# Three stages on one core: v read in 512-byte runs with a swap of key halves, and expert matrices loaded in halves during attention

## The chip, the cores and the metric

The kernel runs on 1 core of a Trainium2 chip. The metric is the device time in microseconds of one execution on that core. All loads and stores are issued by SyncE (SP), in program order, on one DMA queue that 16 DMA engines serve.

## What is computed

Chunked attention over 8 batches, 8 heads, 576 positions and a head size of 64 (chunks of 64 positions attend to themselves alone), then a soft mixture of 8 experts with 4 slots each over all 4608 tokens, then a block of two matrices with softplus between them.

```python
scores = scale * q_c @ k_c^T                      # per chunk of 64
attn = exp(scores - max); attn /= sum + 1e-09
x = attn @ v_c                                    # -> (4608, 512) tokens
logits = x @ phi                                  # 32 slots
d = softmax of logits over the tokens             # dispatch
slot_out[e] = relu((d.T @ x)[e] @ w1[e]) @ w2[e]  # 8 experts, w1: 512x1024, w2: 1024x512
x = softmax of logits over the slots @ slot_out   # combine
out = softplus(x @ w_in) @ w_out                  # 512x2048 and 2048x512
```

## The kernel before

**Attention** runs in 36 units of two heads and 512 positions: 9 groups `G` of four units. Group 0 (`MIXED`) collects the last 64 positions of all batches, group G the first 512 of batch G-1. For a unit, PE transposes q and k (`A0`, `A1`; line 404), ScalarE copies them to the tile `T` (`B`, line 413), GpSimd copies each half of `T` to the other 64 partitions (`M`, line 421), PE makes the scores (`S`, line 435), VectorE takes maximum and difference (`m0`, `m1`; lines 446 and 452), ScalarE the exponential (`x`, line 460), PE transposes the probabilities (`C`, line 468), ScalarE or VectorE copies them back (`Ce`, line 473), PE multiplies them with v (`D`, line 487, into `X`), VectorE normalizes (`n0`, `n1`; lines 501 to 510), PE transposes the result (`E`, line 522) and an engine copies it (`Ee`, line 529). Once a group, `F` (line 540) makes logits and `Fy` (line 598) sums tokens into the slots.

v is loaded for two units at once (`lv`, a pair of units, 512 KB; line 270): four DMAs, one for each block of 128 positions, whose runs in DRAM are one row of 64 floats, that is 256 bytes. Partition p of block m holds position 128m + p. There are three buffers for v; a column of ones behind each head's 64 makes the sum of the probabilities come out of `D`.

**Experts.** `w1` and `w2` have 16 pieces of 1 MB each. `H` n (line 926) multiplies the slots with piece n of w1, `SO` n (line 967) the hidden values with piece n of w2. The pieces lie in slots of SBUF: `w0` to `w7` (each two tiles of 512 KB, loaded by two DMAs), `g0` to `g3` and `i0` to `i3` (one DMA of 1 MB), and `d0` to `d4`, which exist only when the pools of attention are closed, so they wait for the last `A1`, `S` and `D`. Slots are used again: `H` 0 frees `w0` for piece 5 of w2, and so on; `w_in` and `w_out` follow in the slots that come free (`AFTER`).

**What sets the order.** The order on each engine is fixed when the program is built. `issue` keeps a clock for each engine, adds for each step the cost that `COST` lists and a latency, and takes the step that can begin first (at the same time, by rank). Loads of expert pieces (`lw`) have a high rank, so they fill SP's clock where no load of attention can begin. On the chip every engine then works through its list in order, and a step that waits holds up all that stand behind it on its engine.

**After the experts** come `soT`, `Td` (lines 986, 1007) and then 72 blocks of `h` (line 1078), softplus (lines 1097 to 1117) and `o` (lines 1134 to 1138). Beside the experts, three batches of combine weights are made (`c1` to `c6` on VectorE, ScalarE and GpSimd, then `d`, transposes of line 850, and `dc`, copies of line 856), and w_in and w_out are split into two parts each (lines 333 to 350, 872 to 883).

Of the kernel before, what the change touches and what calls it, by code (L numbers as in the profile page):

```python
# [64 lines left out]
class Step:  # L65
    def __init__(self, nm, key, fn, deps, take, give, rank, cost=None, after=()):
# [4 lines left out]
        self.urgent = False  # L71


def issue(steps, buffers, clock=None, held=None):
# [26 lines left out]
    while n:  # L101
# [30 lines left out]
        s.end = clock[e] + LATENCY[e]  # L132
# [10 lines left out]
def kernel(  # L143
# [98 lines left out]
    vb = [vb2[:, i].rearrange("p (m h e) -> p m h e", m=4, e=VW) for i in range(2)]  # L242
    vb += [ap.tile([128, 4, 4, VW], F32, name=f"vb{i}") for i in range(2, NV)]
# [40 lines left out]
    def load(nm, n, sl):  # L284
# [9 lines left out]
        parts = halves(sl)  # L294
        if sl[0] == "w":
            for t, x in zip(parts, (src[:, 0], src[:, 1])):
                nc.sync.dma_start(out=t.bitcast(U32) if nm == "wo" else t, in_=x)
# [83 lines left out]
    def st_lv(pr):  # L381
        def f(e, held):
            if pr // 2 == MIXED:
                assert held["v", pr] == pr
                V["v", pr] = vm[:, :, 4 * pr:4 * pr + 4]
                if pr == 0:
                    load_vm()
                return
            V["v", pr] = vb[held["v", pr]]
            load_v(V["v", pr], pr)  # L390
# [33 lines left out]
    def st_S(u):  # L424
        def f(e, held):
# [4 lines left out]
            for i in range(4):  # L430
                for b in range(2):
                    for h in range(2):
# [3 lines left out]
                            out=sp[64 * o:64 * o + 64, b, 64 * i:64 * i + 64],  # L436
# [12 lines left out]
    def st_m1(u):  # L449
        def f(e, held):  # L450
            t = V["P", u] = ap.tile([128, 4, 128], F32, tag=f"P{held['P', u]}", name="P")
            nc.vector.tensor_tensor(  # L452
# [23 lines left out]
    def st_D(u):  # L476
        def f(e, held):
            xp = V["X", u] = psa.tile([128, 2, 512], F32, tag="X", name="X")
            pt, vt = V.pop(("P", u)), V["v", u // 2]
            for i in range(2):  # L480
                for h in range(2):
                    for b in range(2):
                        m = 2 * b + i
                        for c in range(2):
                            o = c ^ b
                            a = 64 * (h ^ b)
                            nc.tensor.matmul(  # L487
# [916 lines left out]
```

## Time and profile before

| what | us |
|---|---|
| three runs | 680.23, 681.58 (median), 685.54 |
| the profiled execution | 681.11 |
| its span, first to last instruction | 679.3 |
| PE busy over the span | 635.1 |
| VectorE, ScalarE, GpSimd busy | 428.7, 335.6, 237.5 |
| DMA: bytes moved | 107.93 MB, 159 GB/s mean |

Shares of busy time are means over stages that differ: the span has an attention stage (to about 160 us), an expert stage (to about 225 us), a start of the last stage (to about 290 us) and the rest of it. What ends last is read in each stage apart.

### The profile page before, as it was taken

What the parts mean: (1) busy time and instruction counts of PE and PEld (TensorE: products, weight loads), DVE (VectorE), ACT (ScalarE), POOL (GpSimd) and SP (SyncE); (2) the same over time, 40 slices, a digit from 0 to 9 for tenths busy, and PEclk for the clock granted to TensorE, in tenths of its full rate; (3) what the DMA queues carried; (4) which work ended last, traced back from release to release, by engine and by line L of the source; (5) the groups of instructions that cost most, each with busy time, mean ns of one, the idle gap of its engine ahead of it and who ended that gap; (6) DMA issues with size and microseconds to landing.
All of it is one profiled execution on the core that took longest, in us unless ns stands there. A gap on an engine that the chain in (4) does not pass through costs nothing.

```text
span 679.3 us, 14080 instructions
## 1 busy us (share of the span) xinstructions
PE 635.1 (93%) x5831; PEld 510.1 (75%) x5831; DVE 428.7 (63%) x630; ACT 335.6 (49%) x511; POOL 237.5 (35%) x205
## 2 busy tenths in 40 slices
PE   6899889978984899999999999999999999999997
PEld 5787777865352577878788788888888888888885
DVE  1778778774247589878887777754455554545551
ACT  2565656642046589645555865553333333333330
POOL 4233223220214536612222234444333444433341
PEclk7999999998898789999999999999999999999999
DMA  9799989899999802102412510122414223231312
GB/s 176 195 259 257 262 241 271 219 315 418 415 409 415 323 31 95 61 31 99 150 62 90 221 62 32 59 97 73 113 63 123 64 81 106 78 110 63 119 36 62
DMA packets 80255, 107.93 MB, mean 159 GB/s; under 512 B 42432, under 2 KB 60864, under 8 KB 78016
## 3 DMA queue, kind: packets, MB, share of 16 engines
q1 hardware_dynamic: 80192, 107.04, 48.5%
q8 instruction: 46, 0.75, 0.5%
q14 instruction: 17, 0.14, 0.1%
HBM read 88.15 MB, written 18.87 MB: 158 GB/s over the span
## 4 chain that ended last, share of the span: by engine, by line
PE 72%; DMA 13%; DVE 8%; issue 2%; ACT 2%; POOL 2%; SPq 1%; POOLq 0%; DVEq 0%; ACTq 0%
PE trm L1134 17%; PE trm L1136 17%; PE trm L1138 17%; DMA i<-in_moe_w_dram 5%; PE ph L1078 4%; PE tr L404 3%; PE X L487 2%; PE S L435 2%; DMA d<-in_moe_w_dram 2%; PE tr L468 2%; DMA g<-in_moe_w_in_dram 2%; PE tr L522 2%; DMA w5b<-in_moe_w_dram 1%; DMA w3b<-in_moe_w_dram 1%; PE tr L540 1%
## 5 line engine op out<-in xcount | busy, mean ns | idle before, releaser
L1117 POOL TENSOR_TENSOR g<-hTm,g 128x1024 fp32r<-128x1024 f32 (+1 forms) x37 | 87.4, 2363 | 111.7 <-ACT g L1113 107.9
L1103 ACT ACTIVATE hTm<-hTm 128x1024 f32<-128x1024 f32 (+2 forms) x51 | 51.4, 1010 | 78.4 <-DVE hTm L1097 78.1
L1097 DVE TENSOR_SCALAR hTm<-ph 128x1024 uint32<-128x1024 uint32 (+2 forms) x51 | 59.0, 1158 | 35.0 <-PE ph L1078 34.9
L421 POOL COPY T<-T 64x512 f32<-64x512 f32 x72 | 43.9, 610 | 99.7 <-ACT T L413 98.9
L1107 DVE SCALAR_TENSOR_TENSOR hTm<-ph,hTm 128x1024 f32<-128x1024 f32 (+1 forms) x37 | 44.2, 1195 | 25.6 <-ACT hTm L1103 25.5
L1113 ACT CAST g<-hTm 128x1024 fp32r<-128x1024 f32 (+1 forms) x37 | 38.0, 1027 | 40.0 <-DVE hTm L1107 40.0
L1150 DVE TENSOR_TENSOR i<-trm,i 128x512 f32<-128x512 f32 x52 | 35.7, 687 | 31.9 <-PE trm L1138 31.8
L413 ACT COPY T<-tr 128x512 f32<-128x512 f32 x72 | 40.9, 588 | 23.3 <-PE tr L404 23.2
L1078 PEld LDWEIGHTS ph<-cT,Tc 128*128 128x128 f32 x288 | 43.7, 190 | 11.4 <-issue 4.4
L1078 PE MATMUL ph<-cT,Tc 128*128 128x256 f32 x288 | 47.0, 286 | 2.4 <-DVE g L1117 1.2
L1097 DVE TENSOR_SCALAR siT<-ph 128x1024 uint32<-128x1024 uint32 (+1 forms) x25 | 29.5, 1181 | 25.6 <-PE ph L1078 25.5
L1103 ACT ACTIVATE siT<-siT 128x1024 f32<-128x1024 f32 (+1 forms) x25 | 25.7, 1027 | 38.5 <-DVE siT L1097 38.5
L1117 POOL TENSOR_TENSOR g<-siT,g 128x1024 fp32r<-128x1024 f32 x12 | 28.9, 2408 | 42.5 <-ACT g L1113 42.5
L1117 DVE TENSOR_TENSOR g<-ph,g 128x1024 fp32r<-128x1024 f32 (+2 forms) x27 | 29.6, 1102 | 10.0 <-ACT g L1113 10.0
L404 PE MATMUL tr<-ident,q 128*128 128x128 f32 x144 | 29.1, 284 | 5.7 <-DMA q<-in_q_dram 4.3
L446 DVE TENSOR_REDUCE nm<-S 128x8 f32<-128x512 f32 x36 | 24.7, 686 | 14.7 <-PE S L435 14.6
L1113 ACT CAST g<-ph 128x1024 fp32r<-128x1024 f32 (+2 forms) x27 | 24.7, 919 | 18.2 <-DVE ph L1107 16.8
L435 PE MATMUL S<-T 64*64 64x64 f32 x1152 | 25.2, 225 | 6.0 <-DVE P L452 2.8
L435 PEld LDWEIGHTS S<-T 64*64 64x64 f32 x1152 | 21.1, 137 | 12.0 <-issue 7.2
L460 ACT ACTIVATE P<-P 128x512 f32<-128x512 f32 x36 | 23.0, 638 | 11.5 <-DVE P L452 11.4
L404 PE MATMUL tr<-ident,k 128*128 128x128 f32 x144 | 28.3, 279 | 0.3 <-DMA k<-in_k_dram 0.3
L452 DVE TENSOR_TENSOR P<-S,nm 128x512 f32<-128x512 f32 x36 | 24.5, 681 | 2.1 <-PE S L435 1.3
(453 smaller groups left out, 1766.7 us busy)
## 6 DMA issues: line engine op xcount, KB each, us to landing
part<-i SPq DMA_DIRECT2D x18, 512.0 KB, 2.6
i<-part SPq DMA_DIRECT2D x18, 512.0 KB, 3.6
q<-in_q_dram SPq DMA_DIRECT2D x32, 256.0 KB, 4.7
k<-in_k_dram SPq DMA_DIRECT2D x32, 256.0 KB, 4.6
i<-in_moe_w_dram SPq DMA_DIRECT2D x7, 1024.0 KB, 15.5
vbm<-in_v_dram SPq DMA_DIRECT2D x40, 128.0 KB, 4.7
g<-in_moe_w_dram SPq DMA_DIRECT2D x5, 1024.0 KB, 7.9
d<-in_moe_w_dram SPq DMA_DIRECT2D x5, 1024.0 KB, 13.4
```

The source lines that it names most:

```text
L404: nc.tensor.transpose(c, t[:, h, 2 * rr:2 * rr + 2, :].rearrange("p r d -> p (r d)"), ident)
L421: nc.gpsimd.tensor_copy(out=t[a:a + 64, :, 1], in_=t[b:b + 64, :, 2 * h])
L435: nc.tensor.matmul(out=sp[64 * o:64 * o + 64, b, 64 * i:64 * i + 64], lhsT=cs[:, 0], rhs=cs[:, 1], start=True, stop=True)
L1078: nc.tensor.matmul(out=ph(n, a, b)[:, j - a, :], lhsT=K["Tc"][:, f * 128:(f + 1) * 128], rhs=K["cT"][:, t * TT:(t + 1) * TT], start=True, ...
L1097: nc.vector.tensor_scalar(out=scratch(n, a, b).bitcast(U32), in0=ph(n, a, b).bitcast(U32), scalar1=0x80000000, scalar2=None, op0=ALU.bitwi ...
L1103: nc.scalar.activation(out=y, in_=y, func=AF.Softplus)
L1107: nc.vector.scalar_tensor_tensor(out=soft(n, a, b), in0=ph(n, a, b), scalar=0.0, in1=y, op0=ALU.max, op1=ALU.add)
L1113: nc.scalar.copy(out=V["gs", n][:, 0, a:b], in_=soft(n, a, b))
L1117: tt(e)(out=s[:, 1, a:b], in0=soft(n, a, b), in1=s[:, 0, a:b].bitcast(F32), op=ALU.subtract)
L1134: nc.tensor.matmul(out=po, lhsT=s[:, 0, j, ts_], rhs=wr[:, hs], start=(n in begin and j == 0), stop=False)
L1136: nc.tensor.matmul(out=po, lhsT=s[:, 0, j, ts_], rhs=wr[:, ls], start=False, stop=False)
L1138: nc.tensor.matmul(out=po, lhsT=s[:, 1, j, ts_], rhs=wr[:, hs], start=False, stop=(j == 3 and n in finish))
```

## The change

For all groups but `MIXED`, v is read in runs of two rows (512 bytes): two DMAs for a pair of units in place of four, each over 256 positions, with positions 256b + 2p and 256b + 2p + 1 on partition p. A chunk's keys then don't lie where the scores of that chunk have them, so new steps `N` exchange 32 partitions of one of the two rows with 32 of the other, through a buffer of the `xT` tiles: six copies for a pair of units, four on GpSimd and two on ScalarE, one after the other, and `D` waits for them. The order of chunks in `S`, `m1`, `D` and in the stores follows from the new layout; the permuting write in `m1` goes away. The planner's cost of `lv` falls from 2.7 to 2.1, and 2.5 us are added to the time at which it takes v to be there. Each expert piece of the first 11 of w1 that don't wait for attention's pools, and the first five of w2, is loaded as two steps of 512 KB with a cost of 1.35 each (before: one step of 2.6); g and i slots, too, are now filled by two DMAs.

```diff
-    "lq": {"SP": 1.7}, "lv": {"SP": 2.7}, "lwi": {"SP": 1.35},
+    "lq": {"SP": 1.7}, "lv": {"SP": 2.1}, "lwi": {"SP": 1.35},
...
+"N": {"POOL": 0.65},
...
-        s.end = clock[e] + LATENCY[e]
+        s.end = clock[e] + LATENCY[e] + s.lag
...
-        for m in range(4):
+        for b in range(2):
             nc.sync.dma_start(
-                out=t[:, m, :, 0:D],
-                in_=v[batch_of(G), h0:h0 + 4, 128 * m:128 * m + 128, :].rearrange(
-                    "h p d -> p h d"))
+                out=t[:, b, :, 1:2 * D + 1],
+                in_=v[batch_of(G), h0:h0 + 4, 256 * b:256 * b + 256, :].rearrange(
+                    "h (p r) d -> p h (r d)", r=2))
...
+    def st_N(pr, n):
+        def f(e, held):
+            t = V["vt", pr]
+            if n == 0:
+                V["vs", pr] = xp_.tile([128, 512], F32, tag=f"xT{held['xT', ('N', pr)]}", name="xT")
+            vtmp = V["vs", pr].rearrange("p (b h d) -> p b h d", b=2, h=4)
+            i, n_ = divmod(n, 3)
+            lo, up = slice(64 * i, 64 * i + 32), slice(64 * i + 32, 64 * i + 64)
+            dst, src = ((vtmp[lo], t[up, :, :, 1:1 + D]),
+                        (t[up, :, :, 1:1 + D], t[lo, :, :, 1 + D:VW + D]),
+                        (t[lo, :, :, 1 + D:VW + D], vtmp[lo]))[n_]
+            if e == "ACT":
+                nc.scalar.copy(out=dst, in_=src)
+            else:
+                nc.gpsimd.tensor_copy(out=dst, in_=src)
...
+            by["lv", pr].lag = 2.5
+            for n in range(6):
+                add("N", (pr, n), st_N(pr, n), [("lv", pr)] + [("N", (pr, n - 1))] * (n > 0),
...
+                    {"ACT": 0.6} if n % 3 == 2 else {"POOL": 0.67})
...
-        add("D", u, st_D(u), [("Ce", u), ("lv", pr)],
+        add("D", u, st_D(u), [("Ce", u), ("lv", pr), ("N", (pr, 2)), ("N", (pr, 5))],
...
+    def halved(nm, n, sl, r):
+        add("lw", (nm, n, 0), at(load, nm, n, sl, 0), rank=r, cost={"SP": 1.35})
+        add("lw", (nm, n), at(load, nm, n, sl, 1), [("lw", (nm, n, 0))], rank=r, cost={"SP": 1.35})
...
-            add("lw", ("w1", n), at(load, "w1", n, sl), rank=100 + n)
+            halved("w1", n, sl, 100 + n)
     for n in range(5):
-        add("lw", ("w2", n), at(load, "w2", n, W2[n]), rank=130 + n)
+        halved("w2", n, W2[n], 130 + n)
...
-        if t % 2 == 0 and G != MIXED:
-            nc.sync.dma_start(out=out[rows[0]:rows[0] + 128, :], in_=o)
-            return
```

SP, the last loads of attention, before. `w0`, `w1`, `g0`, `g1` and `g2` (5 MB of expert pieces, the last of them in the first row) stand ahead of the last v (vb and vbm are the buffers of v), and `w2a` follows on it:

```order
L300 DMA g2_2789<-in_moe_w1_dram 128x2048
L263 DMA q_2834<-in_q_dram 128x2x256
L263 DMA k_2835<-in_k_dram 128x2x256
L270 DMA vb2_116<-in_v_dram 128x4x64 x4
L297 DMA w2a_2930<-in_moe_w1_dram 128x1024
L297 DMA w2b_2931<-in_moe_w1_dram 128x1024
L297 DMA w3a_3007<-in_moe_w1_dram 128x1024
L297 DMA w3b_3008<-in_moe_w1_dram 128x1024
```

SP, the same place now (line 300 is an expert piece, 264 q and k, 271 v):

```order
L300 DMA w5a_2703<-in_moe_w1_dram 128x1024
L271 DMA vbm_115<-in_v_dram 128x4x128 x2
L264 DMA q_2778<-in_q_dram 128x2x256
L264 DMA k_2779<-in_k_dram 128x2x256
L300 DMA w5b_2704<-in_moe_w1_dram 128x1024
L300 DMA w6a_2860<-in_moe_w1_dram 128x1024
L264 DMA q_2906<-in_q_dram 128x2x256
L264 DMA k_2907<-in_k_dram 128x2x256
L271 DMA vb2_116<-in_v_dram 128x4x128 x2
L300 DMA w6b_2861<-in_moe_w1_dram 128x1024
L302 DMA g3_3024<-in_moe_w1_dram 128x1024
```

Nine more DMAs of 512 KB (`w2a` to `w6a`) stand ahead of the last load of v than before.

GpSimd in the middle of attention, before (line 421 is `M`, two for a unit):

```order
L421 COPY T_798<-T_798 64x16x32 x2
L421 COPY T_855<-T_855 64x16x32 x2
L421 COPY T_943<-T_943 64x16x32 x2
L421 COPY T_1015<-T_1015 64x16x32 x2
L421 COPY T_1113<-T_1113 64x16x32 x2
```

GpSimd in the middle of attention, now (line 447 is `M`, line 414 is `N`, which reads or writes a buffer of v):

```order
L414 COPY xT_1567<-vb2_116 32x512
L447 COPY T_1558<-T_1558 64x16x32
L414 COPY vb2_116<-vb2_116 32x8x64
L447 COPY T_1558<-T_1558 64x16x32
L447 COPY T_1585<-T_1585 64x16x32
L414 COPY xT_1567<-vb2_116 32x512
L447 COPY T_1585<-T_1585 64x16x32
L414 COPY vb2_116<-vb2_116 32x8x64
L447 COPY T_1675<-T_1675 64x16x32 x2
L414 COPY xT_1743<-vbm_115 32x512
```

The copies that the scores wait for now stand in one list with the copies that wait for v.

PE at the start of the last stage, before (line 986 is `soT`, 1007 `Td`, 1078 `h`, 1134 to 1138 `o`; the three groups of the last batch of combine weights, line 850, stand further ahead, among the `SO`):

```order
L986 MATMUL trm_3827<-rep_60,ts 128x128 x2
L1007 MATMUL trm_3846<-g_3639,soT 128x128 x4
L1007 MATMUL trm_3855<-g_3639,soT 128x256 x4
L1078 MATMUL ph<-cT,Tc 128x256
L1007 MATMUL trm_3875<-g_3639,soT 128x128 x4
L1078 MATMUL ph<-cT,Tc 128x256 x7
L1134 MATMUL trm_3915<-w0a,g_3908 128x512
L1136 MATMUL trm_3915<-w0a,g_3908 128x512
```

PE at the same place now (line 1029 is `soT`, 1050 `Td`, 1121 `h`, 893 the transposes of combine weights, 1177 `o`):

```order
L1029 MATMUL trm_3897<-rep_60,ts 128x128 x2
L1050 MATMUL trm_3915<-g_3614,soT 128x128 x4
L1050 MATMUL trm_3921<-g_3614,soT 128x256 x4
L1121 MATMUL ph<-cT,Tc 128x256
L1050 MATMUL trm_3941<-g_3614,soT 128x128 x4
L893 MATMUL trm_3949<-ident,cr 128x128 x4
L1121 MATMUL ph<-cT,Tc 128x256 x2
L893 MATMUL trm_3963<-ident,cr 128x128 x4
L1121 MATMUL ph<-cT,Tc 128x256 x3
L893 MATMUL trm_3980<-ident,cr 128x128 x4
L1121 MATMUL ph<-cT,Tc 128x256 x2
L1177 MATMUL trm_4003<-w0a,g_3997 128x512
```

The three groups of the last batch have moved from among the `SO` to among the first `h`.

## Rows read from the trace of the kernel before

**Rows 1.** Windows of five stages; first row: what the columns are

```profile
core 0: us, PE busy (x) PEld busy (x) DVE busy (x) ACT busy (x) POOL busy (x), PEclk, DMA share, GB/s
14.00:158.00 144.00, 129.47 (x3093) 106.99 (x3095) 108.57 (x243) 83.85 (x179) 42.72 (x70) 0.98 0.90 257
144.00:174.00 30.00, 24.98 (x408) 17.97 (x402) 14.87 (x40) 9.11 (x23) 4.53 (x5) 0.90 1.02 402
174.00:223.00 49.00, 37.37 (x418) 18.63 (x410) 22.96 (x39) 22.39 (x36) 13.18 (x9) 0.92 1.02 412
223.00:235.00 12.00, 9.77 (x56) 7.69 (x56) 5.96 (x14) 6.49 (x15) 4.73 (x4) 0.74 0.96 380
235.00:290.00 55.00, 52.83 (x234) 41.45 (x234) 48.85 (x65) 45.73 (x74) 28.69 (x19) 0.94 0.17 58
```

**Rows 2.** Chain of waits in order of time (start us, us, what)

```profile
143.90 8.01 DMA w3b<-in_moe_w_dram
...
208.05 15.07 DMA i<-in_moe_w_dram
223.17 1.98 PE sops L967 x16
```

**Rows 3.** Timeline of SP's queue (start us, us)

```profile
58.76 0.46 SPq L297 DMA_DIRECT2D w0a<-in_moe_w_dram  x1
...
133.67 0.46 SPq L300 DMA_DIRECT2D g<-in_moe_w_dram  x1
...
135.72 6.22 SPq L270 DMA_DIRECT2D vb<-in_v_dram  x4
142.00 0.91 SPq L297 DMA_DIRECT2D w2a<-in_moe_w_dram  x1
...
174.21 0.33 SPq L297 DMA_DIRECT2D w0a<-in_moe_w_dram  x1
```

**Rows 4.** Timeline of PE (start us, us): four places

```profile
160.41 0.70 PE L487 MATMUL X<-vb,P 64*64 64x65 f32 x32
...
172.25 1.06 PE L926 MATMUL hps<-w0a,siT 128*32 128x512 f32 x2
...
212.40 0.66 PE L850 MATMUL trm<-ident,cr 128*128 128x128 f32 x4
...
235.39 0.50 PE L1134 MATMUL trm<-w0a,g 128*128 128x512 f32 x1 [0.65 <-ACT g L1113]
```

**Rows 5.** Waits of PE and GpSimd in attention (us, times, longest us)

```profile
PE X L487 <- issue: 4.2, 3, 2.1
...
POOL T L421 <- ACT T L413: 98.3, 56, 7.3
```

**Rows 6.** Groups by form in attention (count, busy us, mean ns, idle before)

```profile
L421 POOL COPY T<-T 64x512 f32<-64x512 f32 x70 | 42.7, 610 | 99.1 <-ACT T L413 98.3
...
L473 ACT COPY P<-tr 128x512 f32<-128x512 f32 x21 | 12.2, 587 | 17.7 <-PE tr L468 17.7
...
L473 DVE COPY P<-tr 128x512 f32<-128x512 f32 x14 | 9.6, 689 | 8.2 <-PE tr L468 8.0
```

**Rows 7.** Line 421 (GpSimd's `M`): durations, and who waited for it (us, times)

```profile
L421 POOL COPY T<-T x72: 606/610/616, 5.8 to 148.5; 64x512 f32<-64x512 f32 x72
...
  PEld S L435: 4.0, 7
```

**Rows 8.** Windows of three stretches of DMA traffic (columns as in rows 1)

```profile
6.00:11.00 5.00, 1.45 (x33) 1.13 (x32) 1.38 (x2) 1.21 (x2) 0.96 (x2) 0.64 1.42 169
...
188.00:203.00 15.00, 12.62 (x176) 8.95 (x178) 6.37 (x15) 6.91 (x13) 1.82 (x1) 1.00 1.03 409
152.00:164.00 12.00, 9.88 (x152) 7.03 (x153) 5.17 (x13) 3.05 (x6) 0.00 (x0) 0.86 1.03 419
```

**Rows 9.** Line 270 (load of v)

```profile
DMA to landing us min/median/max: 2.5/4.8/7.9
```

**Rows 10.** Groups of ScalarE by form, 186 to 216 us

```profile
L856 ACT CAST cT<-trm 128x512 fp32r<-128x512 f32 x8 | 5.0, 640 | 10.1 <-PE trm L850 10.0
```

More of the change, by code (lines that the diff above doesn't have):

```diff
@@ L241 @@
     vb2 = ap.tile([128, 2, 16 * VW], F32, name="vbm")
-    vb = [vb2[:, i].rearrange("p (m h e) -> p m h e", m=4, e=VW) for i in range(2)]
-    vb += [ap.tile([128, 4, 4, VW], F32, name=f"vb{i}") for i in range(2, NV)]
+    vb = [vb2[:, i].rearrange("p (b h e) -> p b h e", b=2, e=2 * VW) for i in range(2)]
+    vb += [ap.tile([128, 2, 4, 2 * VW], F32, name=f"vb{i}") for i in range(2, NV)]
     vm = vb2.rearrange("p i (m h e) -> p (i m) h e", m=2, e=VW)
@@ L282, in load_vm, with load @@
                     "x p d -> p x d"))
-    def load(nm, n, sl):
+    def load(nm, n, sl, part=None):
         e, i = divmod(n, 2)
@@ L293, in load @@
             src = w_out_u[256 * n:256 * n + 256, :].rearrange("(k p) f -> p k f", p=128)
-        parts = halves(sl)
+        parts = V["parts", nm, n] if part == 1 else halves(sl)
+        V["parts", nm, n] = parts
         if sl[0] == "w":
-            for t, x in zip(parts, (src[:, 0], src[:, 1])):
-                nc.sync.dma_start(out=t.bitcast(U32) if nm == "wo" else t, in_=x)
+            for i_, (t, x) in enumerate(zip(parts, (src[:, 0], src[:, 1]))):
+                if part in (None, i_):
+                    nc.sync.dma_start(out=t.bitcast(U32) if nm == "wo" else t, in_=x)
+        elif part is not None:
+            nc.sync.dma_start(out=parts[part], in_=src[:, part])
         else:
@@ L388, in f @@
                 return
-            V["v", pr] = vb[held["v", pr]]
-            load_v(V["v", pr], pr)
+            t = V["vt", pr] = vb[held["v", pr]]
+            V["v", pr] = lambda i, b, c, h: t[64 * i:64 * i + 64, b, h, VW * c:VW * c + VW]
+            load_v(t, pr)
+        return f
+    def st_N(pr, n):
[13 more added lines that the diff above has]
+                nc.gpsimd.tensor_copy(out=dst, in_=src)
+            if n == 4 and pr < 2 * MIXED + 2 + NV:
+                nc.gpsimd.memset(t[:, :, :, 0:2 * VW:2 * VW - 1], 1.0)
         return f
@@ L430, in f @@
             for i in range(4):
+                k = i if u // HP == MIXED else i // 2 + 2 * (i % 2)
                 for b in range(2):
@@ L747 @@
     make_identity(nc, ident)
-    for t in vb:
-        nc.gpsimd.memset(t[:, :, :, D:VW], 1.0)
+    nc.gpsimd.memset(vm[:, :, :, D:VW], 1.0)
     for a in range(4):
@@ L1154, in st_oc @@
         G, m = t // 2, 2 * (t % 2) + i
-        if G == MIXED:
-            rows = [(m + 4 * j) * S + GT for j in range(2)]
-        else:
-            rows = [batch_of(G) * S + 128 * m + 64 * j for j in range(2)]
-        if t % 2 == 0 and G != MIXED:
-            nc.sync.dma_start(out=out[rows[0]:rows[0] + 128, :], in_=o)
-            return
-        for j, r in enumerate(rows):
+        for j in range(2):
+            r = (m + 4 * j) * S + GT if G == MIXED else batch_of(G) * S + 64 * (
+                4 * (t % 2) + 2 * j + i)
             p0 = 64 * (j ^ t % 2)
```

49 lines of the change are left out of this document (30 added, 19 removed), and 2 rows, old and new, of the table COST.

## Prediction

> **What bounds the kernel now.** I read the windows by stage first, because the shares over the whole span mix stages with different limits. In attention PE is busy for 129.5 of 144 us, VectorE for 108.6, ScalarE for 83.9, GpSimd for 42.7, and the DMA share is 0.90 at 257 GB/s [rows 1]. From 174 to 223 us it is the other way round: the DMA share is 1.02 at 412 GB/s, and VectorE, ScalarE and GpSimd work for less than half of the time. After 235 us DMA falls to 0.17 and PE is busy again for 52.8 of 55 us.
>
> The chain of waits says the same with an end to each stage: from 143.9 us it is an unbroken row of six waits for DMAs, and its last one, for a piece of w2, ends at 223.1, where the last `SO` starts at once [rows 2]. So from SP's first load after attention, at 142.0 [rows 3], until 223.1 the kernel is a queue of bytes. Seven issues from 58.8 to 133.7 us bring 5 MB of expert pieces during attention [rows 3]; 30 MB are left for the time after it (11 MB of w1, 16 MB of w2, 2 MB of w_in, 1 MB of w_out). At 412 GB/s, 1 MB takes 2.545 us, and 30 take 76.4 of the 81.1 us that I see; the other 4.7 us are the last load of v, still under way, and the start of the queue.
>
> In attention no wait of PE names a DMA; what the waits of PE hold is "issue", 4.2 us on `D` in three pieces [rows 5]. GpSimd waits 98.3 us for ScalarE there. DMA is busy but not late.
>
> **More expert bytes in attention.** Nine pieces of 512 KB now stand ahead of the last load of v: 4.72 MB, at 412 GB/s **-11.45 us** in the stage that DMA bounds. Taken from the end of attention the same sum reads: 25.5 MB are left, 142 + 4.7 + 25.5 x 2.545 = 211.6 in place of 223.1.
>
> Is something else late by then? Piece 5 of w2 goes into `w0` and waits for the first `H`. Before, SP issued it at 174.21, when the `H` that began at 172.25 was through [rows 3, 4]. In the new order 11.5 MB stand ahead of it, so the queue runs until 142 + 4.7 + 29.3 = 176.0, 1.8 us after that issue, and a DMA takes at least 2.5 us from issue to landing [rows 9]. The two just meet. Before, the queue had some 11 us to spare here; now each microsecond by which attention ends later is a microsecond of the total. The `d` pieces meet the last `D` (160.4 to 161.1 [rows 4]) in the same way: 6.5 MB stand ahead of the first piece that waits for it, 142 + 4.7 + 16.5 = 163.2. I take the gain whole, and count attention's length apart.
>
> **v in longer runs.** This buys DMA time, not time of the chain, since PE doesn't wait for v. While v came almost alone in 256-byte runs, the queue moved 169 GB/s [rows 8], that is 24.2 ns for a run on one of 16 engines; with long runs it moves 412, 159 ns for 4 KB. A line through both gives 33.2 ns for 512 bytes, an estimate, or 247 GB/s: 2.12 us for the 512 KB of a pair of units in place of 3.10. Over 16 pairs that is 15.7 us of DMA time freed against 11.45 us added, so the share in attention goes from 0.90 to about 0.87. The ends are 169 GB/s (nothing freed) and 412 (29 us freed).
>
> [...] No row of this case has a 512-byte run. [...]
>
> Smaller pieces for `g` and `i` cost nothing that I can see: a stretch with mostly 512 KB pieces ran at 409 GB/s, one with 1 MB pieces at 419 [rows 8], and the SP issues are 0.3 to 0.5 us each [rows 3], beside transfers of 1.3 us. For v SP issues two DMAs less a pair. The 16 stores that become two wait for nobody, beside a DMA share of 0.17 in the stage after 235 us [rows 1].
>
> **The swap.** Four copies on GpSimd for each of 16 pairs: 64 x 0.610 = 39 us [rows 6]; with its 42.7 GpSimd is busy for 82 of 144 us. Two on ScalarE: 32 x 0.587 = 18.8 us; the planner in turn moves seven of the copies `Ce` and `Ee` to VectorE (30 there before, 37 now), so ScalarE gets 14.7 us more, to 98.5, and VectorE 7 x 0.689 = 4.8 more, to 113.4. All four stay under 144, and PE's list has the same matmuls as before.
>
> Yet the lists are worked off in order. Behind an `N` that waits for v or for the other engine's `N` stand on GpSimd the `M` that the scores wait for, and on ScalarE the copies and exponentials. Bounds for attention: at the lower end -4.2 us, if PE's "issue" waits came from a crowded DMA; at the upper end VectorE's 4.8 us and one copy of 0.61 us on the path for each pair, 9.8, together 14.6. In the rows, `M` held up the scores seven times in 72, for 4.0 us, on the weight loads that run ahead of PE [rows 7]. Doubling GpSimd's work about doubles this, and half of it is covered: **+2 us**, nearest to that row.
>
> **The last batch of combine weights.** Its three groups of transposes were done by 213 us [rows 4], under DMA waits. Now they stand among the first `h`, in the 12 us between the last `SO` and the first `o` (235.39 [rows 4]), where nothing covers them: 3 x 0.66 = 2.0 us of PE and 3 x 0.64 = 1.9 us of ScalarE [rows 4, 10]. Bounds: 0 (PE waits there for VectorE and ScalarE anyway) and 3.9. I take **+1.5**, since ScalarE is what the first `o` waits on in that row.
>
> **Sum**, against the profiled execution of 681.1 us (span 679.3; median of the runs 681.58): 681.1 - 11.45 + 2 + 1.5 = **673.1**, in round terms 673. About 1%, 6.8 us, is what a measurement of this kernel tells from no change; the edge lies at 674.8.
>
> **Rivals.**
> A, the forecast: 673, with its own range 669.5 to 677 from the bounds of the two small terms. 0.52.
> B, relief: with fewer runs DMA is idle often enough that "issue" waits shrink and the tail costs nothing: 681.1 - 11.45 - 2.5 = 667. For it, the DMA share of 0.90; against it, that those waits name no DMA. 0.12.
> C, 512-byte runs move no faster than 256-byte ones. Then 11.45 us are added to a queue that has some 14 us to spare, q and k come late in places, and about half of the gain is given back: 679. Against it, 169 beside 412 GB/s, which shows a price for each run. 0.10.
> D, **slower**: the swap holds up the scores. The mechanism is one `N` on GpSimd that waits for ScalarE's `N`, or for v, with an `M` behind it; PE then stands in each of 16 pairs. The break-even is (11.45 - 1.5) / 16 = 0.62 us a pair, one GpSimd copy. With two copies, 1.22 us, 19.5 us are lost: 681.1 - 11.45 + 1.5 + 19.5 = 691. For it, the chain of six steps over two engines; against it, three buffers of v and 98 us of idle GpSimd [rows 5]. 0.15, half of it beyond 1%.
> E, the bytes land at 212 but the arithmetic doesn't follow: the conversion of w_in and the combine batches have 11 us less to hide in. With the 3.9 us above and one round of a batch, 2 us more: 681.1 - 11.45 + 2 + 5.9 = 677.5. 0.11.
>
> **How the numbers follow.** Faster by over 1%: two thirds of A and all of B, 0.35 + 0.12, and a little of E: 0.48. Slower by over 1%: half of D, 0.07. The rest is 0.45. The range reaches from the upper side of B, 666, to the lower half of D, 685; what lies beyond is about half of B and a third to a half of D.
>
> **What will show it.** In the trace of the changed kernel: the last wait for a w2 piece ends near 212 to 214, and the waits before it begin at about 142 as now; the DMA share in attention is not above 0.95; the first `H` starts within 3 us of 172.25; waits of the scores for GpSimd's copy are below 10 us; the three groups of transposes stand between the last `SO` and the first `o`, which comes some 14 us after the last piece lands. Wrong it is if the first `H` comes at 178 or later (D or C, told apart by who is waited for), or if the last piece lands at 212 and the first `o` is still at 230 or later (E).

## The result and the profile after

The changed kernel takes **686.34 us** (median of 20 runs, 683.25 to 691.66) beside 682.36 us for the kernel before on the same chip (20 runs, 679.24 to 686.11). The ratio is 1.0055, with a 95% interval from 1.0031 to 1.0079: about 4 us slower, where 8 us of gain were forecast, and 1.3 us beyond the upper end of the range. Its profiled execution has a span of 681.5 us, near the lower end of its runs; that of the kernel before had 679.3.

The windows of the changed kernel, with the columns and the first three stages of [rows 1], and one more window of its own:

```profile
14.00:158.00 144.00, 128.29 (x2961) 105.93 (x2965) 105.82 (x235) 95.98 (x194) 79.84 (x134) 0.98 0.88 271
144.00:174.00 30.00, 25.93 (x555) 19.71 (x553) 19.70 (x49) 16.16 (x37) 10.59 (x18) 0.89 0.88 317
174.00:223.00 49.00, 43.61 (x485) 24.62 (x483) 21.68 (x49) 16.77 (x32) 12.42 (x8) 0.93 1.01 396
...
160.00:184.00 24.00, 19.10 (x262) 13.88 (x262) 10.10 (x30) 7.06 (x20) 3.60 (x3) 0.86 0.81 298
```

By 158 us the queue has moved more than before (271 GB/s for 257) at a slightly lower share, as forecast. But PE has begun 2961 matmuls by then, not 3093, and from 144 to 174 us PE still has 555 to do in place of 408. Attention is late. The queue, full in that stage before (1.02), is now partly idle: 0.81 from 160 to 184 us.

SP's timeline says why:

```profile
147.23 0.96 SPq L271 DMA_DIRECT2D vb<-in_v_dram  x2
...
164.92 0.80 SPq L305 DMA_DIRECT2D d<-in_moe_w_dram  x2
...
173.25 0.80 SPq L305 DMA_DIRECT2D d<-in_moe_w_dram  x2
...
184.67 0.33 SPq L300 DMA_DIRECT2D w0a<-in_moe_w_dram  x1
```

The last load of v goes out at 147.23 (135.72 before, [rows 3]). The moved bytes are in early, but what comes next waits for memory that attention holds: the last `d` pieces for the last `D`, until 173.25, and piece 5 of w2 for the first `H`, until 184.67 (174.21 before).

Four places of PE's timeline, which answer to [rows 2] and [rows 4]:

```profile
183.57 0.62 PE L969 MATMUL hps<-w0a,siT 128*32 128x512 f32 x2
...
226.14 1.09 PE L1010 MATMUL sops<-i,hTm 128*32 128x256 f32 x16 [1.43 <-DMA i<-in_moe_w_dram]
...
234.64 0.60 PE L893 MATMUL trm<-ident,cr 128*128 128x128 f32 x4
...
239.57 0.50 PE L1177 MATMUL trm<-w0a,g 128*128 128x512 f32 x1 [2.30 <-ACT g L1156]
```

The first `H` comes 11.32 us later than before, and the last `SO` 2.97 us later. Between the two lie 42.57 us, before 50.92, so this stretch is 8.35 us shorter, and what goes before it 11.32 longer. The rest of the kernel is 0.8 us shorter (455.4 us from the last `SO` to the end of the span, 456.1 before). The sum, +11.32 - 8.35 - 0.8, is the 2.2 us between the spans.

The chain of waits of the changed kernel, in order of time:

```profile
183.64 2.76 PE hps L969 x24
186.51 11.70 DMA g<-in_moe_w_in_dram
...
204.24 11.48 PE sops L1010 x176
...
217.83 1.81 POOL cr L886
219.68 1.09 PE trm L893 x8
```

Before, this stretch was a row of waits for DMAs. Now it is one DMA, then PE's own matmuls and a copy on GpSimd for the combine weights.

### The profile page after: what moved, and what is told of

It is laid out like the page before. It is cut to its first block, busy times and chain, and to the rows that moved or that the text cites. A ratio compares the mean times of both kernels' runs of the same rounds, so it can differ in the third digit from the quotient of the medians.

```text
span 681.5 us, 14213 instructions
## 1 busy us (share of the span) xinstructions
PE 636.5 (93%) x5831; PEld 512.8 (75%) x5831; DVE 430.4 (63%) x640; ACT 349.1 (51%) x533; POOL 276.7 (41%) x270
## 4 chain that ended last, share of the span: by engine, by line
PE 82%; DVE 8%; DMA 3%; issue 3%; ACT 2%; POOL 1%; SPq 1%; DVEq 0%; POOLq 0%; ACTq 0%
PE trm L1179 18%; PE trm L1177 18%; PE trm L1181 18%; PE ph L1121 5%; PE tr L430 4%; PE X L519 3%; PE S L462 3%; PE tr L555 3%; PE tr L501 2%; PE sops L1010 2%; DMA g<-in_moe_w_in_dram 2%; PE tr L631 1%; DMA q<-in_q_dram 1%; PE tr L573 1%; DVE cvt L338 1%
## 5 line engine op out<-in xcount | busy, mean ns | idle before, releaser
L1156 ACT CAST g<-hTm 128x1024 fp32r<-128x1024 f32 (+1 forms) x37 | 38.0, 1027 | 39.8 <-DVE hTm L1150 39.8
L462 PE MATMUL S<-T 64*64 64x64 f32 x1152 | 26.7, 224 | 12.8 <-issue 6.4
L462 PEld LDWEIGHTS S<-T 64*64 64x64 f32 x1152 | 22.2, 136 | 18.4 <-issue 10.7
L493 ACT ACTIVATE P<-P 128x512 f32<-128x512 f32 x36 | 22.7, 631 | 15.9 <-DVE P L480 10.7
L501 PE MATMUL tr<-ident,P 128*128 128x128 f32 x144 | 23.4, 286 | 3.4 <-ACT P L493 2.0
```

The costliest lines, as they stand in the source:

```text
L462: nc.tensor.matmul(out=sp[64 * o:64 * o + 64, b, 64 * k:64 * k + 64], lhsT=cs[:, 0], rhs=cs[:, 1], start=True, stop=True)
L1156: nc.scalar.copy(out=V["gs", n][:, 0, a:b], in_=soft(n, a, b))
```

## The experiments

"Matmuls" are PE's matmuls begun from 14 to 80 us, by the window of that stretch; "first H" and "last SO" are starts in PE's timeline; "issue" is the sum of PE's waits named issue from 14 us to the first `H`. "Old lists" means that the planner's prices were chosen so that PE's list in attention is row for row that of the kernel before. The column "lists" names the order in which PE, VectorE and ScalarE work up to the first `H`: O is that of the kernel before, A that of the changed kernel, B and C are two others (shown below). Each row has one profile; the ratios are from timed runs, each against runs of the kernel before made beside them. The profiled executions of e1 and e3 took 4.6 and 4.3 us longer than the median of their kernels, that of e7 3.3 us less.

| kernel | lists | median us | ratio to before (95%) | matmuls | first H | last SO | issue us |
|---|---|---|---|---|---|---|---|
| before | O | 682.36 | 1 | 1420 | 172.25 | 223.17 | 7.5 |
| before, second profile (e15) | O | | | 1409 | 180.21 | 226.58 | 8.8 |
| changed | A | 686.34 | 1.0055 (1.0031 to 1.0079) | 1182 | 183.57 | 226.14 | 8.5 |
| changed, second profile (e16) | A | | | 1258 | 182.52 | 226.24 | 10.7 |
| e1 changed, no swap copies | A | 685.49 | 1.0023 (0.9984 to 1.0061) | 1159 | 190.41 | 233.09 | 14.0 |
| e2 changed, pieces as before | B | 689.48 | 1.0094 (1.0063 to 1.0125) | 1286 | 180.48 | 230.44 | 8.5 |
| e3 changed, neither | B | 690.51 | 1.0117 (1.0044 to 1.0191) | 1178 | 187.81 | 237.92 | 12.3 |
| e4 before + halves moved by v's price | C | 690.32 | 1.0087 (1.0049 to 1.0125) | 1277 | 184.46 | 229.22 | 12.1 |
| e5 before + v's price alone | C | 690.27 | 1.0114 (1.0048 to 1.0180) | 1284 | 183.21 | 230.31 | 10.3 |
| e6 old lists, moved halves | O | 687.13 | 1.0057 (1.0020 to 1.0094) | 1407 | 183.92 | 227.53 | 15.1 |
| e7 old lists, runs | O | 682.10 | 0.9977 (0.9938 to 1.0016) | 1412 | 173.98 | 219.69 | 5.2 |
| e8 old lists, runs, swap, moved | O | 687.61 | 1.0066 (1.0028 to 1.0105) | 1280 | 185.52 | 231.95 | 11.0 |
| e9 old lists, runs, moved | O | 684.87 | 1.0047 (1.0019 to 1.0076) | 1340 | 180.54 | 225.67 | 11.3 |
| e10 old lists, runs, swap | O | 686.05 | 1.0043 (1.0006 to 1.0080) | 1320 | 178.28 | 227.84 | 3.7 |
| e11 old lists, no piece ahead of v | O | 688.95 | 1.0101 (1.0064 to 1.0138) | 1417 | 170.65 | 232.34 | 4.2 |
| e12 old lists, nine loads of 4 KB | O | 683.00 | 1.0014 (0.9981 to 1.0046) | 1417 | 175.79 | 222.84 | 10.1 |
| e13 changed, `d` pieces behind | A | 685.78 | 1.0046 (1.0018 to 1.0074) | 1175 | 188.16 | 229.08 | 12.4 |
| e14 as e8, `d` pieces behind | O | 687.62 | 1.0066 (1.0033 to 1.0098) | 1285 | 188.56 | 231.71 | 10.3 |

(In e13 and e14 the last two groups of `SO` stand in one row, whose start is given.)

**First four: the swap, or the moved pieces?** e1 takes the copies out of the changed kernel, e2 the moved halves, e3 both; e4 gives the kernel before the halves alone.

```diff
 e1, e3:
-            if e == "ACT":
-                nc.scalar.copy(out=dst, in_=src)
-            else:
-                nc.gpsimd.tensor_copy(out=dst, in_=src)
 e2, e3:
-            halved("w1", n, sl, 100 + n)
+            add("lw", ("w1", n), at(load, "w1", n, sl),
+                [("lv", NU // 2 - 1)] if n > 4 else [], rank=100 + n)
...
 e4, to the kernel before (with halved() of the change):
-    "lv": {"SP": 2.7}
+    "lv": {"SP": 2.1}
-            add("lw", ("w1", n), at(load, "w1", n, sl), rank=100 + n)
+            halved("w1", n, sl, 100 + n)
...
```

> The changed kernel without the 96 copies that exchange the key halves (they are left out, so the second and fourth quarter of the keys stand in each other's place); v still comes in 512-byte runs, the moved expert halves and the order of all other work stay. Theory S (the swap copies, worked off in order on GpSimd and ScalarE, are what lengthens attention): the first H is back within 3 us of 172.3 (before 172.25, changed kernel 183.57), the last w2 wait ends at 212 to 215, time 672 to 677, ratio to before about 0.985 to 0.99. Theory L (19 expert halves among q, k and v crowd the queue, so units start late): first H stays at 180 or later, time 683 or more, ratio 1.00 or above. Theory P (the planner's new order of everything else): as L, first H at 180 or later.

> The changed kernel with 512-byte runs and swap, but with the expert matrices as before: whole pieces, five of them ahead of the last load of v, the rest behind it. Theory S: attention is still long, first H at 180 to 184, the last load of v at about 147 and with it the queue of bytes 11 us later, time 690 to 694, ratio 1.013 to 1.018. Theory L: first H at 171 to 175, time 680 to 684, ratio about 1.00.

> 512-byte runs alone: no swap copies (left out, the key halves aren't exchanged) and expert matrices as before. Theories S and L both: first H at 170 to 174, time 679 to 683, ratio 1.00; with the DMA queue relieved perhaps 1 to 2 us less. Theory P: first H at 178 or later although neither suspect is there, time 686 or more.

> The kernel before with one part of the change: expert pieces in separate halves, and the planner's cost of a load of v lowered to that of the change, which puts 19 halves ahead of the last load of v, as in the changed kernel. v in 256-byte runs, no swap. Theory S: first H at 172 to 176 (the 256-byte runs leave the DMA share near 0.97, so a little late), the bytes land at 212 to 216, time 672 to 678, ratio 0.985 to 0.995. Theory L: first H at 180 or later, DMA share near 1, time 684 or more.

Neither S nor L holds alone. Every one of the four has its first `H` at 180 or later and none is faster than the kernel before; e3, with neither suspect in it, is among the slowest. What the four share is the price of 2.1 us for a load of v, by which the planner writes all lists. That gave theory P: the lists.

**The lists.** e5 changes that one number in the kernel before. e6 to e8 go the other way: they keep 2.7 and PE's old list, and put the parts of the change in at no price in the plan.

```diff
 e5, to the kernel before:
-    "lv": {"SP": 2.7}
+    "lv": {"SP": 2.1}
 (pieces from the sixth on: behind the last load of v, as they were)
 e6, to the kernel before (e8 has it too):
+        if sl[0] == "w" and n >= 10:
+            for j in range(2):
+                i = 2 * (n - 10) + j
+                add("lw", ..., at(load, "w1", n, sl, j), ... [("lv", 6 + i)] if i < 9 ...,
+                    rank=2 * (6 + i) + 1.25 if i < 9 else 100 + n,
+                    cost={"SP": 0.0 if i < 9 else 1.3})
 e7, to the changed kernel: no steps N, "lv" 2.7, loads as before
 e8, to the changed kernel ("lv" 2.7):
-            by["lv", pr].lag = 2.5
+            by["lv", pr].lag = 0.5
-                    {"ACT": 0.6} if n % 3 == 2 else {"POOL": 0.67})
+                    {"ACT": 0.0} if n % 3 == 2 else {"POOL": 0.0})
```

> The kernel before with one number changed: the price of a load of v by which the planner writes the lists of all engines, 2.7 to 2.1 us, as in the change. v in 256-byte runs, no swap, five whole expert pieces ahead of the last load of v. Theory P (the four runs so far share only this number; by it each list puts steps of the next units ahead of steps that could go, because the plan has q, k and v there earlier than they land): first H at 177 or later, the first exponential near 15 us in place of 10.0, time 686 to 692, ratio 1.007 to 1.015. Rival Q (the lists are as good as before; what costs is anything new in the DMA queue, longer runs of v or moved pieces): first H at 171 to 174, ratio 1.00.

> The kernel before with nine expert halves issued one behind each load of v from the seventh on, at no price in the plan, so that the attention lists of PE, VectorE, ScalarE and GpSimd stay row for row as before; 19 halves stand ahead of the last load of v, as in the change. v in 256-byte runs, no swap. Theory P: first H at 172 to 176 (the DMA share goes to about 0.97, so a little late), last w2 wait ends at 212 to 216, time 672 to 678, ratio 0.985 to 0.995. Rival Q: first H at 179 or later, ratio 1.00 or above.

> The kernel before with v in 512-byte runs and nothing else: the swap is left out of plan and program (the key halves aren't exchanged), PE's and ScalarE's lists are row for row as before, expert pieces as before. Theory P: first H at 169 to 173, time 677 to 682, ratio 0.995 to 1.00, DMA share in attention about 0.8. Rival Q: first H at 177 or later, ratio 1.007 or above, as the runs with the new lists.

> The whole change with the lists of before: v in 512-byte runs, the swap copies on GpSimd and ScalarE, nine expert halves moved into attention, but copies and halves at no price in the plan and a load of v at 2.7 again, so that PE's list is row for row as before and the copies stand in the other lists where v is due. Theory P: first H at 172 to 177, last w2 wait ends at 212 to 216, time 672 to 679, ratio 0.985 to 0.997. Theory S in a weaker form (copies that wait for v with scores' copies behind them): first H at 179 or later, waits of the scores for GpSimd above 10 us, ratio 1.00 or above. Rival Q: the same time, with waits that name no GpSimd.

P is right about e5, and about e7 but for a first `H` 1 us later than expected. The number alone costs 1.1%. And e3 and e7 do the same work, long runs with neither swap nor moved halves, on lists B and on the old: 1.0117 and 0.9977, so lists B cost some 1.4%. Their windows from 14 to 80 us, e3 and then e7:

```profile
14.00:80.00 66.00, 53.69 (x1178) 44.65 (x1177) 37.34 (x81) 36.14 (x72) 19.14 (x34) 0.94 0.81 249
```

```profile
14.00:80.00 66.00, 60.97 (x1412) 50.91 (x1412) 47.99 (x107) 38.72 (x80) 20.81 (x34) 0.97 0.81 238
```

At the same DMA share PE has begun 234 matmuls fewer, at e7's 21.4 a microsecond 10.9 us. In the table every kernel with new lists stands at 1159 to 1286 there, those with old lists and no swap at 1340 to 1420, and those with old lists and the swap at 1280 to 1320. (Lists in another order have other matmuls first, so the counts are only a rough measure of progress.)

P is wrong about e6 and e8. On the old lists, too, the moved halves gain nothing, and the whole change on them (e8) is as slow as the change itself. So lists as good as the old ones would not have been enough.

Nor are the lists of e3 and e5 those of the changed kernel. Windows from 0 to the first `H`, of the kernel before (O), the changed kernel (A), e2 (B) and e5 (C):

```profile
0.00:172.25 172.25, 149.48 (x3315) 123.08 (x3316) 116.33 (x264) 90.69 (x193) 51.44 (x105) 0.96 0.91 264
0.00:183.57 183.57, 155.27 (x3315) 126.41 (x3315) 119.42 (x271) 106.47 (x218) 90.91 (x170) 0.95 0.87 266
0.00:180.48 180.48, 154.14 (x3315) 125.68 (x3316) 114.62 (x258) 111.71 (x231) 90.91 (x170) 0.99 0.82 256
0.00:183.21 183.21, 153.58 (x3315) 123.66 (x3315) 119.52 (x272) 90.04 (x185) 51.34 (x105) 0.95 0.89 256
```

PE begins the same 3315 matmuls in each, but VectorE has 264, 271, 258 and 272 instructions there and ScalarE 193, 218, 231 and 185 (32 copies of the swap are in the second and third). e2 and e3 share one order, e4 and e5 another. Taking the moved halves out of the changed kernel thus rewrote its lists as well, and a step from e3 to e1, or from e2 to the changed kernel, changes two things. Where the work is the same, lists A cost nothing that can be told apart from lists O: 1.0055 beside 1.0066 (the changed kernel and e8), 1.0023 beside 1.0047 (e1 and e9), 1.0046 beside 1.0066 (e13 and e14), each difference with an interval of about 0.45% to each side. Lists A without the moved halves were not run. The granted clock, on average 0.96, 0.95, 0.99 and 0.95 of full speed in these windows, does not explain the late `H` either.

**One part at a time on the old lists.** e9 has e7 and the moved halves, e10 has e7 and the swap. e11 takes away even the five pieces that the kernel before loads in attention, e12 puts nine loads of 4 KB where e6 had nine of 512 KB.

```diff
 e9: e7 with the loads of e6
 e10: e8 with the loads of the kernel before
 e11, to the kernel before:
+            if n < 5:
+                add("lw", ("pad", n), lambda e, held: None, rank=100 + n)
+            add("lw", ("w1", n), ..., [("lv", NU // 2 - 1)] if n < 5 else [], rank=100 + n)
 e12, to the kernel before:
+        nc.sync.dma_start(out=V["parts", "w1", n][j][0:16, 0:64], in_=moe_w1[e, 0:16, 0:64])
...
```

> v in 512-byte runs and nine halves moved into attention, PE's list as before; the swap is left out (the key halves aren't exchanged and the sums' ones aren't restored). Theory B (bytes: with 256-byte runs the queue had no room for 4.7 MB more, 11.5 us of it, so the moved halves alone made attention as much longer; the 15 us that longer runs free make room for them): first H at 173 to 177, last SO at 209 to 214, time 671 to 677, ratio 0.98 to 0.99. Theory I (instructions: more bytes ahead in the queue make PE wait for its instructions, whatever the runs are): PE's waits named issue at 10 us or more against 5.2 without the moved halves, first H at 180 or later, ratio 1.00 or above.

> v in 512-byte runs with the swap copies, expert pieces as before (ten halves ahead of the last load of v), PE's list row for row as before. Theory S (copies worked off in order hold up the scores; e7 without them had the first H at 174): first H at 179 or later, waits for GpSimd and ScalarE above 6 us, time 686 or more, ratio 1.006 or above. Theories B and I: first H at 173 to 176, time 680 to 684, ratio 1.00.

> The kernel before without any expert piece ahead of the last load of v: the five pieces (5 MB) that were issued during attention come behind it, with their places in the plan kept, so that all lists are as before. Theory B: attention is 8 to 13 us shorter (first H at 159 to 164), and the time is 678 to 685, since what the queue loses after attention it gains in it. Theory I: PE's issue waits fall to 5 us or less and first H comes at 166 to 170, time 687 to 692, ratio 1.008 to 1.015. If attention is bound by PE's own list: first H at 171 or 172, time 692 to 695, ratio 1.015 to 1.02.

> The kernel before with nine loads of 4 KB at the places in SP's list where the nine halves of 512 KB stood that were moved with the old lists (e6, first H at 183.9); the pieces themselves come where they came before. Theories B and I: the bytes cost, not the number of loads: first H at 171 to 174, time 680 to 684, ratio 1.00. Rival (SP's list: each more load makes SP wait for one of a few places, so q, k and v go out later): first H at 178 or later, ratio 1.006 or above.

On the old lists the swap costs 0.66% (e10 to e7: 1.0043 to 0.9977), some 4.5 us; with intervals of about 0.4% to each side this is just resolved. The moved halves cost 0.70% there (e9 to e7), with an interval of 0.48%. It is their bytes and not their number: e12 is at 1.0014. With both, e8 is only 0.2% slower than either; the reading, not tested by itself, is that whichever makes attention late first, the second adds little. So on lists O the swap and the moved halves lead from 0.9977 to 1.0066, which covers the 1.0055 of the changed kernel without any of its lists. e11 shows the other side of the balance: without the first five pieces the first `H` is 1.6 us earlier than in the earlier profile of the kernel before, and the time 1.0% longer. The first 5 MB were worth loading there; the next 4.7 MB are not.

Against what was expected, e9 came out as theory I had it and not B. e10 lies between its two expectations, with a first `H` of 178.28 and 1.0043. e11 has the issue waits and the ratio of theory I, and a first `H` 0.65 us later. e12 has the ratio that B and I shared, and a first `H` 1.8 us later than they had.

Where PE waits in e9, which has no swap (us, times, longest):

```profile
PE X L519 <- issue: 3.1, 3, 1.5
PE S L462 <- issue: 2.7, 2, 2.4
PE tr L555 <- issue: 2.5, 2, 1.4
PE tr L573 <- issue: 2.4, 2, 1.9
```

and in e10, which has no moved halves:

```profile
PE tr L501 <- ACT P L493: 2.7, 5, 1.6
PE X L519 <- issue: 2.3, 1, 2.3
```

The moved bytes bring waits named issue, 11.3 us for 5.2 without them: 6.1 of the 6.6 us by which the first `H` is later in e9 than in e7. It is the same on short runs (e6 15.1; the kernel before and e12 7.5, 8.8 and 10.1) and beside the swap (e8 and e14 11.0 and 10.3; e10 3.7). The swap brings waits of the transposes `C` for the exponential. ScalarE's timeline in e10 shows the longest of them, 1.62 us on PE at 34.98, from the other side:

```profile
32.30 0.62 ACT L412 COPY vb<-xT 32x512 f32<-32x512 f32 x1 [2.23 <-POOL vb L414]
33.65 0.62 ACT L412 COPY vb<-xT 32x512 f32<-32x512 f32 x1 [0.73 <-POOL vb L414]
34.30 0.63 ACT L493 ACTIVATE P<-P 128x512 f32<-128x512 f32 x1
```

ScalarE stands before its `N` until GpSimd's is done, with the exponential behind it: 14.0 us in 15 waits in e10, but 0.9 us in one wait in the changed kernel, whose lists were written with the copies.

**The gate, and the scatter.** In the changed kernel the `d` pieces that wait for the end of attention stand among w2 pieces that wait for nothing. e13 puts them behind; e14 does so on e8. e15 and e16 are second profiles of the two kernels.

```diff
-            add("lw", ("w1", n), at(load, "w1", n, sl), deps, rank=110 + n)
+            add("lw", ("w1", n), at(load, "w1", n, sl), deps + [("lw", ("w2", 4))], rank=110 + n)
```

> The changed kernel with one more order: the five d pieces, which wait for the end of attention, go out behind the five w2 pieces that wait for nothing, where they now stand among them and hold SP up. Theory G (the gate: in the changed kernel 5 MB stand behind the last D and 15 MB behind the first H, and the queue idles at a share of 0.81 from 160 to 184 us, some 4.6 us): DMA share from 160 to the first H near 1, last SO 3 to 5 us earlier against the first H (38 to 40 us behind it in place of 42.6), time 681 to 684, ratio to before 0.997 to 1.003 in place of 1.0055. Rival (PE's own work between first H and last SO sets those 42.6 us, or the d pieces are now late for H): ratio 1.004 or above, last SO still 42 us or more behind the first H.

> The same order of pieces on the whole change with the lists of before (e8: ratio 1.0066, first H at 185.5, last SO at 231.95, DMA share 0.79 from 160 to 184). Theory G: last SO 39 to 42 us behind the first H in place of 46.4, ratio 0.998 to 1.003. Rival: ratio 1.005 or above, 45 us or more.

> The kernel before, a second profile, to see how far attention moves between two executions. If its length is steady: first H within 1 us of 172.25, PE's issue waits within 1 us of 7.5. If the waits for instructions scatter: issue waits at other sizes on the same places of PE's list, first H 2 to 5 us away.

> The changed kernel, a second profile: first H at 183.6 within 1 us if attention's length is steady, 2 to 5 us away if the waits for instructions scatter; in both cases at 178 or later.

The order works as meant and gains nothing that can be told apart (1.0046, 1.0066). In e13 the queue is full where it idled, and PE waits for no DMA from the first `H` on. Its window, its waits from 188 to 231 us, and the end of its `SO`:

```profile
160.00:184.00 24.00, 19.65 (x339) 14.57 (x341) 12.01 (x32) 9.18 (x24) 4.13 (x7) 0.86 1.02 412
```

```profile
PE trm L893 <- POOL cr L886: 4.8, 2, 3.0
PE sops L1010 <- ACT hTm L1000: 0.2, 1, 0.2
```

```profile
226.33 2.82 PE L893 MATMUL trm<-ident,cr 128*128 128x128 f32 x12 [2.98 <-POOL cr L886]
229.08 2.20 PE L1010 MATMUL sops<-i,hTm 128*32 128x256 f32 x32
```

The last two groups of `SO` start 40.9 us after the first `H`, the last of them alone some 42, as in the changed kernel, although their bytes are there (in e14 the two start after 43.2). They stand in PE's list behind transposes of combine weights, which wait for GpSimd. So theory G falls: with no wait of PE for a DMA the stretch still takes some 41 to 43 us. That the arithmetic alone sets this, as its rival had it, is not shown. The chain of waits in e13 still goes through a DMA, with conversions on VectorE and copies on GpSimd behind it:

```profile
198.27 7.22 DMA w2b<-in_moe_w_dram
```

And the last batch of combine weights stands ahead of the last `SO` in e13 (in the 12 transposes above), as in the kernel before, where the changed kernel has it behind.

The second profile of the kernel before was the surprise:

```profile
84.25 0.37 PE L404 MATMUL tr<-ident,k 128*128 128x128 f32 x1 [3.26 <-issue]
...
180.21 1.07 PE L926 MATMUL hps<-w0a,siT 128*32 128x512 f32 x2
...
226.58 1.09 PE L967 MATMUL sops<-i,hTm 128*32 128x256 f32 x16 [1.32 <-DMA i<-in_moe_w_dram]
```

Its first `H` is 7.96 us later than in the execution from which I predicted, yet its last `SO` only 3.41 us. One wait for issue of 3.26 us makes a large part of the delay. That delay is more than either of the two expectations for e15 had. The changed kernel's two profiles differ by 1.05 us there. So single profiles of these kernels can differ by several microseconds in attention, and the kernels above are to be judged by their ratios, not by their first `H`.

## Why the prediction was wrong

**The step that failed is the length of attention**, the term "+2 us" under "The swap", in which the moved bytes had no share. It measured +11.3 against the same profile, or 2.3 to 11.3 over the four pairs of profiles. I priced the operations of the swap, and gave the moved bytes no price in attention at all, because "DMA is busy but not late". On the old lists, with the order of PE and VectorE held fixed, both have one: the moved halves 0.70% (some 4.8 us, e9 to e7), the swap 0.66% (some 4.5 us, e10 to e7), and both together bring the kernel to 1.0066 (e8), beside 1.0055 for the change. What the moved bytes bring is PE's waits named issue; what the swap brings on these lists is ScalarE's stand before its `N`. On the changed kernel's own lists the swap costs 0.3% (e1 to the changed kernel), with an interval of 0.45%, so not told apart from nothing.

My own bounds for attention, -4.2 and 14.6 us, held the measured length. The range did not go as far as they do: 681.1 - 11.45 + 14.6 + 3.9 is 688, and I ended it at 685.

Of PE's list I said that it "has the same matmuls as before". It has, in another order, and I took the planner's new number for a load of v for a detail of the edit. On lists B and C the order cost 1.4 and 1.1% (e3, e5), so it needed a term. But it is not what made the changed kernel slow, as far as the runs go: its own lists A are no slower than lists O with the same work (e8, e9, e14).

One place shows what another order does. ScalarE's timeline, first of the kernel before and then of the changed one:

```profile
9.97 0.63 ACT L460 ACTIVATE P<-P 128x512 f32<-128x512 f32 x1 [3.34 <-DVE P L452]
13.92 0.59 ACT L413 COPY T<-tr 128x512 f32<-128x512 f32 x1 [3.32 <-PE tr L404]
```

```profile
15.27 0.58 ACT L439 COPY T<-tr 128x512 f32<-128x512 f32 x1 [8.20 <-PE tr L430]
15.75 0.63 ACT L493 ACTIVATE P<-P 128x512 f32<-128x512 f32 x1
```

In the new list a copy of the next unit, whose q lands only at 14 us, stands ahead of the first exponential, and ScalarE stands there for 8.20 us. By the seventh exponential all but 1.6 us of this is made good.

The reason that I gave for the small term, twice the waits of the scores for GpSimd's `M`, came out nearly as said. In the changed kernel the weight loads of the scores waited for GpSimd's `M` and, in the second row, for its `N`:

```profile
  PEld S L462: 5.4, 9
  PEld S L462: 2.2, 3
```

Together that is 7.6 us for 4.0 before [rows 7]. It was right, and it was not what made attention late. Rival D, an `N` on GpSimd with an `M` behind it, did not happen in its size of 19.5 us; e10 and e8 show its mirror image, on ScalarE, on lists that were not written for it.

**The bytes, -11.45.** The size was too large: the stretch from the first `H` to the last `SO` is 8.35 us shorter than in the same profile, 2.65 to 8.35 over the four pairs. On the old lists there is next to nothing: 45.1 us with the moved halves (e9), 45.7 without (e7). I had written that the queue and the first `H` "just meet"; the condition held, and attention missed it. There is a second limit, near what I gave 0.11 as rival E: in e13 the stretch takes 41 to 43 us although PE waits for no DMA. Before, 50.9 us lay there, or 46.4 in the second profile, and this surplus was a buffer that swallowed the scatter of attention: 7.96 us late cost 3.41. In the changed kernel the buffer is nearly spent (42.6 and 43.7 us). It ends at 226.1, where the kernel before ends in its second profile, at 226.6.

**v in longer runs.** Right. On the same lists the share to 158 us fell from 0.90 to 0.85 while the rate rose from 257 to 269 GB/s (e7). At the old rate for each unit of share, 269 GB/s would have taken 0.94, so 13 us of DMA time came free; 15.7 were forecast. The traces' records of single packets of the queue, from 14 to 158 us, give less: a packet of 256 bytes took 19.4 ns on average in the kernel before and one of 512 bytes 28.7 in e7, which is 39.8 and 29.4 us of all 16 engines, so 10.4 us. A packet of 4 KB took 159 ns there (median), so 512-byte runs move 17.8 bytes a nanosecond on an engine where long ones move 25.8. And e7 shows that this buys no time, as said: 0.9977, which includes 1.

**The combine weights, +1.5.** Their three groups stand among the first `h` as the order said, but the part behind the last `SO` is 0.8 us shorter, so they cost nothing there. In e13, whose list has them ahead of the last `SO` again, they are part of what it waits for.

**The other rivals.** B had waits named issue shrinking. On the old lists they do with long runs and no moved halves (e7, 5.2 us, e10, 3.7), but go to 10 to 15 us with moved halves (e6, e8, e9, e14). C had half of the gain given back by late q and k, 679; all of it was lost and 4 us more, and not by that cause: from 14 us to the first `H` PE has a single wait in the changed kernel that names q or k, at 14 us.

**What stays open.** Which rows of lists B and C cost their 1.1 to 1.4% was not found. Nor is the changed kernel's own attention resolved row by row: beside the first profile of the kernel before, the lasting loss arises between 44 and 80 us, and half of the 11.3 us does not show as waits. Up to the first `H`, PE is busy for 155.27 us in place of 149.48 for the same 3315 matmuls, and as the ends of matmuls are modelled, what this holds is not known. PE's issue waits are 8.5 and 10.7 us in its two profiles, little more than the 7.5 and 8.8 before, but 14.0 and 12.4 in e1 and e13, which have its lists. No version tried beats the kernel before; the best, e7, leaves work out and is not told apart from it.

## What to carry to other kernels

Before moving work out of a stage that a queue bounds, find what the first work behind it waits for and how much of the queue stands behind that gate: only the slack between the two can be gained, and it may be the buffer that hides scatter. Profile the kernel before twice: a stage whose end moves by 8 us between two executions can't be costed to 2 us from one. And where a planner writes in-order lists from prices, one price is a change of its own: compare the order of the lists and not what stands in them, and measure each edit on lists that are held fixed. Here even taking loads out of the changed kernel rewrote its lists, and a path of single steps from kernel to kernel would have laid the loss to the wrong one.

## What the hardware showed beside this

PE's waits named issue are not spread at random: they fall on a grid in PE's own list. Windows from 0 to the start of the matmul that had waited, in e6 and then in the second profile of the kernel before; the first two counts are PE's matmuls and weight loads:

```profile
0.00:62.74 62.74, 51.23 (x1097) 42.85 (x1098) 36.40 (x79) 31.88 (x62) 21.60 (x59) 1.00 0.89 212
0.00:70.18 70.18, 56.87 (x1223) 47.60 (x1223) 41.80 (x90) 35.45 (x69) 24.05 (x63) 1.00 0.91 229
0.00:88.34 88.34, 72.39 (x1599) 60.36 (x1599) 53.82 (x118) 45.97 (x94) 28.95 (x71) 1.00 0.91 238
...
0.00:128.05 128.05, 105.72 (x2352) 86.94 (x2353) 80.98 (x178) 67.28 (x137) 39.36 (x88) 0.99 0.91 244
```

```profile
0.00:69.35 69.35, 56.94 (x1223) 46.94 (x1223) 40.81 (x89) 35.72 (x69) 23.95 (x63) 0.93 0.89 219
0.00:84.25 84.25, 68.29 (x1472) 56.14 (x1473) 50.63 (x111) 42.97 (x85) 27.00 (x68) 0.93 0.88 223
0.00:123.99 123.99, 105.51 (x2353) 87.30 (x2354) 80.89 (x178) 66.96 (x136) 39.20 (x88) 0.93 0.86 227
```

The sums for e6 are 2195, 2446, 3198 and 4705: steps of 251, 752 and 1507, that is 1, 3 and 6 times 251. The other kernel has 2446, 2945 and 4707, on the same grid. All 137 waits of PE named issue between 14 us and the first `H`, in all 18 profiles, fall on it to within an eighth of a step. Which places of it wait, and how long, changes from run to run; e6 waits for 1.80 us at the place of 2446, before there was no wait in the first profile and one of 0.44 us in the second. With the profile page's row of the queue that it names instruction,

```profile
q8 instruction: 46, 0.75, 0.5%
```

46 packets of together 0.75 MB, 16 KB each, which the page counts on the same 16 engines as the data, the reading is that PE waits at the start of a block of its own instructions. PE's 5831 matmuls and as many weight loads make 46.5 steps of 251. The packet records of the first profiles of the kernel before and of the changed kernel fit it: all 46 packets of this queue have 16,384 bytes, one lands for 249 of PE's matmuls and weight loads on average, and PE's 14 waits named issue between 14 us and the first `H`, seven in each, end 1.3 to 1.6 us after one of them landed. Over the 18 profiles these waits add up to 3.7 to 15.1 us, in an attention of some 160. That the wait is longer because data is queued on the same engines fits e11 (4.2 us with no piece), the kernel before (7.5 and 8.8 with 5 MB) and e6 (15.1 with 9.7 MB), and the pairs e7 and e9, e10 and e8; with 10.1 us in e12, at 5 MB, the scatter is too large to call it shown.
